# Block products after Strassen's scheme for two of the matrix products of a gated MLP behind windowed attention

## The chip, the core and the metric

The kernel runs on one core of a Trainium2 chip. Its engines are named as in the profile: PE is TensorE, DVE is VectorE, ACT is ScalarE, POOL is GpSimd, and SP is the queue that issues the DMAs. The metric is the device time of one execution in microseconds (us); smaller is better.

## The reference

Windowed causal attention with a linear bias by distance, over 8 batches of 8 heads (576 positions, 64 numbers a head), and behind it, on the 512 numbers a position that the heads give together, a gated MLP with a residual. Cut to what is computed:

```python
scores = scale * q @ k.T                       # 8 batches, 8 heads, 576 x 576
scores = where((rel >= 0) & (rel < 128), scores + bias, -1e9)
x = softmax(scores) @ v                        # per batch: 576 x 512 over all heads
h = gelu(x @ w_in)                             # w_in 512 x 1024
u, v = h[..., :512], h[..., 512:]
v_n = (v - mean) / sqrt(var + 1e-6) * g_ln
v_s = einsum('ts,bsd->btd', w_sg, v_n) + b_sg  # w_sg 576 x 576
return x + (u * v_s) @ w_out                   # w_out 512 x 512
```

## The kernel before

**Number format.** TensorE is fed with rounded fp32 (`fp32r`). To keep more digits, each operand of the MLP is held as a high part and a low part, the low part being what the rounding left over. A product is then three matmuls into the same PSUM tile: high by high, high by low, low by high. The helper `mm3` issues them from three lines, L567, L568 and L569, so these lines appear for every matrix product of the MLP. The split itself is a cast on ACT (high) and a subtraction on POOL or DVE (low).

**Attention.** Two heads make a pair of 128 partitions; there are 32 pairs, four to a batch. A pair `n` is a row of steps with letters: loads `q`, `L` (SP); scores `*` (PE, L248); `A B C G` (DVE: mask, bias, row minimum; L267, L274); `e E f F j` (ACT: exponentials, L283); `R` (DVE: inverse sums); `r s S` (POOL: scaling, L304); transposes `t T` (PE, L314); `X Y` (DVE: copies with a mask, two instructions each, L323); `z P 2 p` (the first 64 positions); `V` (PE: values, L352); `x h k` (ACT: gather, high part, tail of the low part); `l` (POOL: low part, L366).

**MLP of batch b.** The products are kept transposed, features on the partitions. `tt` and `v` give the half that is normalised (moving operand 512 wide), `vg`, `nv..`, `vn` its gelu, mean, variance and split. `u` gives the other half: four blocks of 128 features by two halves of 288 positions, 12 matmuls each, 96 in all; `uc` (ACT, L697) takes a block out of PSUM and `ug` is its gelu. `y` is the product with `w_sg`, and `gm` (DVE, L720) multiplies it out of PSUM with u. `gh` (ACT, L724) and `gl` (POOL, L727) split the gated result. `O` is the product with `w_out`, again 96 matmuls of 288; `oa` (DVE, L750) adds it out of PSUM to the residual, and `D` stores it.

**Order.** One string, `ORDER`, lists all steps of all batches; each engine runs its own steps in that order, and the framework places the semaphores. Attention steps of the next batch stand between the MLP steps of the one before, except in the last batch, where nothing is left to stand between. PSUM has two buffers for each of three uses (`ps_s`, `ps_a` attention, `ps_m` MLP). An MLP tile in `ps_m` is two banks of 288 or 512.

**Buffers.** `vn` (normalised v, high and low) and `g` (gated result, high and low) have places of their own; `u` is a tile of its own; `xs` is x in two parts, four tiles; `xf` is the residual, eight tiles.

Of the kernel before, what the change touches and what calls it, by code (L numbers as in the profile page):

```python
# [21 lines left out]
def attention_gmlp(  # L22
# [402 lines left out]
    xfs, xss = [{} for _ in range(B)], [{} for _ in range(B)]  # L425
# [15 lines left out]
    def add_pair(n):  # L441
# [35 lines left out]
        put("p", "ACT", 0.2, [f"2{n}"], take=[("xf", [f"D{b}{c}"])])  # L477
# [98 lines left out]

    def add_norm(b, key, at, after, rows, done, his, lo):
# [19 lines left out]
        def high():  # L597
            x["hi"] = his()
            for h in x["hi"]:
                nc.scalar.activation(h, x["vg"][0:rows], AF.Copy, scale=x["rs"][0:rows])  # L600

        def low():
            nc.vector.scalar_tensor_tensor(out=lo(), in0=x["vg"][0:rows], scalar=x["rs"][0:rows], in1=x["hi"][0].bitcast(F32), op0=ALU.mult, op1=ALU.subtract)
# [6 lines left out]
        add(k + "h", "ACT", 1.25 if key == "t" else 0.63, at, high, [k + "p", k + "c"] + ([f"y{b - 1}{f}{i}" for f in range(NF) for i in range(2)] if b else [f"-{c}" for c in range(2 * NC)]))  # L610
        add(done, "DVE", 0.68, at, low, [k + "h"], port=True)

    def add_mlp(b):
# [55 lines left out]
        def add_v(t2, at):  # L669
            for i in range(2):  # L670
                t = t2 + i
                take = [("ps_m", [f"vg{b}{t2}", f"vg{b}{t2 + 1}"])]
                if b == 0:
                    for c in range(NC):
                        add(f"w{t}{c}" if c < NC - 1 else f"v{b}{t}", "PE", 0.75, pair_at(c) + OPEN, v_sum(t, [c]), [f"h{c}", f"l{c}", f"-{c}", f"H{c}", f"w{t}{c - 1}" if c else None, f"w{t2}0" if i else None], take=take if c == 0 and i == 0 else [])
                else:
                    add(f"v{b}{t}", "PE", 2.82, at + 2.82 * STRETCH * i, v_sum(t, range(NC)), rows + ([f"v{b}{t2}"] if i else []), take=take if i == 0 else [])
            for i in range(2):
                last = at + 2.82 * STRETCH * i
                add(f"vg{b}{t2 + i}", "ACT", 0.51, last - AHEAD, gelu_v(t2 + i), [f"v{b}{t2 + i}"], table="g", take=[("vg", [f"vn{b}{t2 + i}"])])  # L680
                add_norm(b, f"v{t2 + i}", last, [f"vg{b}{t2 + i}"], P, f"vn{b}{t2 + i}", lambda t=t2 + i: [vn()[:, 0, t, :]], lambda t=t2 + i: vn()[:, 1, t, :])

        def add_u(f, at):
# [10 lines left out]
            def copy():  # L694
                if f == 0:
                    st["u"] = mlp.tile([P, NF, S], F32, name="u")
                nc.scalar.copy(in2(st["u"][:, f, :]), st[f"pu{f}"][:, :, 0:S2])  # L697
# [3 lines left out]
            add(f"uc{b}{f}", "ACT", 0.55, at - AHEAD, copy, [f"u{b}{f}1"] + ([f"uc{b}0"] if f else []), take=[] if f else [("u", [f"gl{b}{k}" for k in range(NF)])])  # L701
            if f == NF - 1:
                add(f"ug{b}", "ACT", 2.05, at, lambda: nc.scalar.activation(st["u"], st["u"], AF.Gelu_apprx_tanh), [f"uc{b}{k}" for k in range(NF)], table="g")

        def add_y(f, at):
            fs = slice(f * P, (f + 1) * P)

            def sums(i):
                def run():
                    if i == 0:  # L710
                        st[f"py{f}"] = ps_m.tile([P, 2, 512], F32, name="ps_m")
                    y, ss, vn, vA = st[f"py{f}"][:, i, 0:S2], halves[i], st["vn"], st["vA"]
                    mm3(y, [((vn[:, 0, t, fs], vn[:, 1, t, fs]), (ws[:, 0, t, ss], ws[:, 1, t, ss])) for t in range(T)], last=False)
                    nc.tensor.matmul(y, vA[:, fs], wsA[:, ss], start=False, stop=False)  # L714
                    nc.tensor.matmul(y, vB[:, fs], wsB[:, ss], start=False, stop=True)  # L715
                return run

            def gate():
                u = st["u"][:, f, :]
                nc.vector.tensor_tensor(in2(u), st[f"py{f}"][:, :, 0:S2], in2(u), ALU.mult)  # L720

            def high():
                st[f"g{f}"] = mlp.tile([P, 2, S], F32R, name="g", bufs=NF)
                nc.scalar.activation(st[f"g{f}"][:, 0, :], st["u"][:, f, :], AF.Copy)  # L724

            def low():
                nc.gpsimd.tensor_tensor(st[f"g{f}"][:, 1, :], st["u"][:, f, :], st[f"g{f}"][:, 0, :].bitcast(F32), ALU.subtract)  # L727

            for i in range(2):
                need = [f"tn{b}", f"nt{b}h"] + [f"vn{b}{t}" for t in range(T)] + (["t-", "b-", "tH"] + [f"w-{c}" for c in range(T)] if b == 0 else [])  # L730
                add(f"y{b}{f}{i}", "PE", 1.87, at + 1.87 * STRETCH * i, sums(i), need + ([f"y{b}{f}0"] if i else []), take=[] if i else [("ps_m", [f"gm{b}{f}"])])
            add(f"gm{b}{f}", "DVE", 0.69, at - AHEAD, gate, [f"y{b}{f}1", f"ug{b}"])
            add(f"gh{b}{f}", "ACT", 0.6, at - AHEAD, high, [f"gm{b}{f}"] + (["bH", "tl"] + [f"i{8 + c}" for c in range(NF)] if b == 0 else []), take=[("g", [f"O{b}{c}" for c in range(NC)])])
            add(f"gl{b}{f}", "POOL", 1.39, at - AHEAD, low, [f"gh{b}{f}"])

        def add_o(c, at):
# [11 lines left out]
            def total():  # L748
                o = x[c]
# [12 lines left out]
            add(f"D{b}{c}", "SP", 0.5, at, lambda: nc.sync.dma_start(out[b, cs, :], x[c]), [f"oa{b}{c}"], lag=2.5)  # L762
# [126 lines left out]
```

## Time and profile before

| what | value |
|---|---|
| median of 3 runs (632.78 to 634.25) | 633.5 us |
| the profiled execution: its own time | 634.58 us |
| its span, first to last instruction | 632.9 us |
| so outside the span | 1.7 us |
| granted TensorE clock, mean | 0.995 |
| instructions | 14839 |
| DMA traffic | 57.24 MB |

A busy share in the profile is the time in which an engine had an instruction running, over the span. For PE the ends of instructions are modelled, since matmuls overlap in its pipeline; the distance from one start to the next is the better measure of what a matmul costs. A row of a group names line, engine and operation, output and input tiles, the shape, the count, then the busy time, the mean of one in ns, and the idle time of the engine ahead of these instructions with what ended it. A row of waits names who waited for whom, the sum in us, how many times, and the longest.

### The profile page before, as it was taken

The page shows a single profiled execution, that of the slowest core. Times are in us where ns is not written, and L with a number is a line of the kernel's source. Part 1 is how long each engine was busy: PE and PEld are TensorE (multiplying, and loading weights), DVE is VectorE, ACT ScalarE, POOL GpSimd, SP SyncE. Part 2 cuts the span into 40 slices and gives each one's busy share as a digit, 9 for nine tenths or more (in the row PEclk, how much of TensorE's full clock was granted, in tenths as well). Part 3 has the DMA queues.
Part 4 walks back from the last instruction along what each step waited for, and adds up shares of the span by engine and source line. Part 5 has one row for each costly group of instructions (what it writes and reads, how often), then busy time and mean ns, then how long its engine had stood idle before and what let it go on. Part 6 is the DMA issues. An engine that isn't in the chain of part 4 may idle for free.

```text
span 632.9 us, 14839 instructions
## 1 busy us (share of the span) xinstructions
PE 602.5 (95%) x5664; PEld 549.7 (87%) x5664; DVE 379.7 (60%) x1297; ACT 369.6 (58%) x1079; POOL 224.6 (35%) x229
## 2 busy tenths in 40 slices
PE   2799899999999999999999999999999999999997
PEld 1577799898999899998999889998899879998896
DVE  4899887465664664548545676546845486633511
ACT  7999687845653467447664586439354465733330
POOL 3666533623073303624053140722325141450220
PEclk9999799999999999999999999999999999999999
DMA  7786321212321520342221422134023512000003
GB/s 249 246 267 217 116 73 46 71 40 79 114 58 42 153 78 2 104 143 99 78 60 40 152 78 78 48 111 150 1 78 103 168 38 80 3 2 20 1 1 132
DMA packets 55931, 57.24 MB, mean 90 GB/s; under 512 B 8498, under 2 KB 45362, under 8 KB 55860
## 3 DMA queue, kind: packets, MB, share of 16 engines
q1 hardware_dynamic: 55860, 56.28, 28.3%
q8 instruction: 45, 0.74, 0.5%
q14 instruction: 26, 0.21, 0.1%
HBM read 46.83 MB, written 9.44 MB: 89 GB/s over the span
## 4 chain that ended last, share of the span: by engine, by line
PE 80%; DVE 8%; ACT 8%; issue 2%; DMA 1%; POOL 1%; POOLq 0%; SPq 0%; ACTq 0%; DVEq 0%
PE ps_m L567 19%; PE ps_m L569 18%; PE ps_m L568 18%; PE ps_s L352 7%; PE ps_a L314 4%; PE ps_s L248 4%; PE ps_a L248 3%; ACT e L283 2%; DVE px L323 2%; PE ps_m L714 1%; PE ps_m L715 1%; ACT e L302 1%; PE ps_m L651 1%; PE ps_m L653 1%; DMA qk<-qkT 1%
## 5 line engine op out<-in xcount | busy, mean ns | idle before, releaser
L283 ACT ACTIVATE e<-e,stats 128x128 f32<-128x128 f32 (+1 forms) x320 | 121.1, 381 | 29.2 <-DVE stats L267 28.8
L304 POOL TENSOR_TENSOR e<-e,rr 128x512 f32<-128x512 f32 (+1 forms) x88 | 73.6, 851 | 129.9 <-DVE rr L296 113.6
L567 PE MATMUL ps_m<-xs,wi 128*128 128x288 f32 x256 | 79.1, 309 | 3.0 <-ACT vg L641 1.8
L567 PE MATMUL ps_m<-ws,vn 128*128 128x288 f32 x256 | 78.2, 306 | 0.0
L567 PE MATMUL ps_m<-g,wo 128*128 128x288 f32 x256 | 78.2, 305 | 0.0
L568 PE MATMUL ps_m<-xs,wi 128*128 128x288 f32 x256 | 76.0, 297 | 0.0
L569 PE MATMUL ps_m<-xs,wi 128*128 128x288 f32 x256 | 76.0, 297 | 0.0
L569 PE MATMUL ps_m<-g,wo 128*128 128x288 f32 x256 | 75.8, 296 | 0.0
L568 PE MATMUL ps_m<-ws,vn 128*128 128x288 f32 x256 | 75.6, 295 | 0.0
L569 PE MATMUL ps_m<-ws,vn 128*128 128x288 f32 x256 | 75.4, 295 | 0.0
L568 PE MATMUL ps_m<-g,wo 128*128 128x288 f32 x256 | 74.9, 293 | 0.5 <-POOL g L727 0.5
L592 POOL TENSOR_TENSOR rs<-rs,mhalf 128x1 f32<-128x1 f32 (+1 forms) x40 | 30.5, 763 | 125.8 <-DVE rs L589 115.1
L366 POOL TENSOR_TENSOR xs<-xf,xs 128x576 fp32r<-128x576 f32 x32 | 45.4, 1427 | 53.3 <-ACT xs L363 51.3
L727 POOL TENSOR_TENSOR g<-u,g 128x576 fp32r<-128x576 f32 x32 | 45.5, 1423 | 50.7 <-ACT g L724 50.6
L323 DVE TENSOR_TENSOR px<-ps_a,m_old 128x512 f32<-128x512 f32 x64 | 43.6, 682 | 31.8 <-PE ps_a L314 21.8
L283 ACT ACTIVATION_READ_ACCUMULATOR e<-e,stats 128x1 f32 (+1 forms) x320 | 60.4, 189 | 0.0
L567 PEld LDWEIGHTS ps_m<-xs,wi 128*128 128x128 f32 x256 | 48.8, 191 | 8.8 <-ACT vg L641 2.5
L750 DVE TENSOR_TENSOR xf<-ps_m,xf 128x576 f32<-128x576 f32 x32 | 23.7, 749 | 52.4 <-PE ps_m L569 52.3
L567 PE MATMUL ps_m<-wi,xs 128*128 128x512 f32 x128 | 52.4, 409 | 1.4 <-ACT vg L641 1.4
L248 PE MATMUL ps_s<-qk 64*64 64x192 f32 (+2 forms) x632 | 40.3, 344 | 14.2 <-DMA qk<-qkT 10.3
L352 PE MATMUL ps_s<-px,vt 128*64 128x128 f32 (+1 forms) x972 | 51.2, 259 | 0.3 <-DVE px L323 0.2
L352 PEld LDWEIGHTS ps_s<-px,vt 128*64 128x64 f32 x972 | 47.2, 137 | 3.9 <-issue 2.1
(120 smaller groups left out, 1522.0 us busy)
## 6 DMA issues: line engine op xcount, KB each, us to landing
qk<-qkT SPq DMA_DIRECT2D x32, 576.0 KB, 4.1
vt<-v_in SPq DMA_DIRECT2D x64, 256.0 KB, 3.4
outT<-xf SPq DMA_DIRECT2D x32, 288.0 KB, 2.8
wst<-w_in SPq DMA_DIRECT2D x8, 512.0 KB, 5.0
vt<-v_in SPq DMA_DIRECT2D x64, 32.0 KB, 2.9
wst<-w_out SPq DMA_DIRECT2D x4, 512.0 KB, 4.5
wst<-w_sgT SPq DMA_DIRECT2D x4, 288.0 KB, 6.0
vd<-v_in SPq DMA_DIRECT2D x64, 16.0 KB, 2.9
```

The source lines that it names most:

```text
L248: return lambda: nc.tensor.matmul(dst, qk[js, 0, q0:q0 + R], qk[js, 1, k0:k1], start=True, stop=True)
L283: nc.scalar.activation(x, x, AF.Exp, bias=self.nm[0:n, i:i + 1], scale=-1.0, accum_out=self.sm[0:n, i:i + 1])
L304: nc.gpsimd.tensor_tensor(x, x, self.rr[0:n, i:i + m].rearrange("p (m o) -> p m o", o=1).broadcast_to([n, m, c]), ALU.mult)
L314: burst([lambda t=t: nc.tensor.transpose(ct[:, t * P:(t + 1) * P], self.pr[j][:, t, :], ident) for t in range(T)])
L323: nc.vector.tensor_tensor(xv[:, :, :, i, :], cv, m.rearrange("p (t h c) -> p t h c", t=1, h=1).broadcast_to([P, T, 2, R]), ALU.mult)
L352: return lambda: nc.tensor.matmul(x1[heads[j], q0 + lo // 2 * R if t < 0 else q0 + t * R:q0 + (hi + 1) // 2 * R], block, px[j][:, (half * ...
L366: nc.gpsimd.tensor_tensor(lo_of(self.xs), self.xf, hi_of(self.xs).bitcast(F32), ALU.subtract)
L567: nc.tensor.matmul(dst, ah, bh, start=(first and i == 0), stop=False)
L568: nc.tensor.matmul(dst, ah, bl, start=False, stop=False)
L569: nc.tensor.matmul(dst, al, bh, start=False, stop=(last and i == n - 1))
L592: nc.gpsimd.tensor_tensor(x["rs"][0:rows], x["rs"][0:rows], mhalf[0:rows], ALU.pow)
L727: nc.gpsimd.tensor_tensor(st[f"g{f}"][:, 1, :], st["u"][:, f, :], st[f"g{f}"][:, 0, :].bitcast(F32), ALU.subtract)
```

## The change

The products `O` of batches 1 to 7 and `u` of batches 2 to 7 are cut into 2 by 2 blocks (weights 256 by 256, moving side 256 by 288) and formed from seven block products in place of eight. A block product is 12 matmuls of 288 columns (two row blocks, two inner blocks, three for the parts). The constant `FAST = 2` says from which batch `u` is done this way. Batch 0 keeps both old forms, batch 1 keeps the old `u`.

What that takes, by step names (`b` is the batch, `n` the number of the block product, 1 to 7):

- `U{b}{n}` and `O{b}{n}` (PE): the block products. They share two PSUM tiles. Products 1, 6, 7, 4 go through the one and 5, 3, 2 through the other; 6, 7, 4 and 3 are added to what is in the tile, and each product is taken out before the next goes into the same tile.
- `ue` (four on ACT, three on DVE) and `oa` (seven on DVE, in place of four) take them out. Their row length is again 576.
- `ut` (4 a batch) and `gt` (4 a batch): differences of blocks of x and of the gated result, on DVE from SBUF to SBUF. `uh`, `ul` and `gh`, `gl` split them; that is 4 splits a batch that were not there for `u`, and 7 in place of 4 for `O`. `gl6` is on DVE, the others on POOL; two of them a batch (`gl1`, `gl2`) and `ul6` are cut in two instructions.
- Sums of weights, once: `Us0`..`Us9` on POOL and `ks0`..`ks9` on DVE (128x512 each), `Uh`, `kh` (8 on ACT) and `Ul`, `kl` (8 on DVE) for the split. Three of the four sums of a matrix stay in three tiles `sum`; the fourth replaces a block of the weights. Both matrices use the same three tiles, so the sums are stored in DRAM (`Ud`, `kd`: 6 stores of 512 KB) and loaded back when the other matrix is at work (`lu`, `lo`: 18 loads of 512 KB each). The loads stand in SP's queue with those of q, k, v and the stores of the output.
- Buffers: `vn` and the split blocks share one tile `region` of four slots, with a fifth slot in `g` and `spare`. So a block of the gated result may only be written when `y` has read the part of `vn` in that slot, and `vn` of the next batch only when the block product that reads the slot is done. `u` and the residual (two sets for even and odd batches) are fixed tiles.
- The first two `y` of a batch are cut in two (`ya` over the first half of the positions, then `y`), `v` of batches 2 to 7 is cut around the `U`, and `D` stores a block of 256 by 288, four a batch as before.
- `ORDER` is written anew.

Counted in the two programs, PE has 4418 instructions before and 4262 after, DVE 1299 and 1415, ACT 761 and 814, POOL 234 and 302, SP 279 and 321. (The weight loads of PE are not in these counts, and the profile counts some small matmuls of the attention twice; those of 288 columns are the same in both.)

The diff, cut to its core:

```diff
+    store = [dram.tile([P, 3, 2, 2, 2 * P], F32, name=f"store{i}") for i in range(2)]
+    def load_sums(i, number):
+        return lambda: nc.sync.dma_start(sums[i].bitcast(F32), store[number][:, i])
...
+    SLOT_USE = {0: 5, 1: 6, 2: 4, 3: 7}
...
+        def add_fast_u(at):
+            def less(n, a, c):
+                return lambda: nc.vector.tensor_tensor(u(*place[n]), a, c, ALU.subtract)
+            def put(n):
+                add(f"uh{b}{n}", "ACT", 0.69, at, high(n), [f"ut{b}{n}"] + freed[n])
+                add(f"ul{b}{n}", "POOL", 1.42, at, low(n), [f"uh{b}{n}"])
...
+            def product(n, key, first):
+                def run():
+                    if key not in st:
+                        st[key] = ps_m.tile([P, 2, 512], F32, name="ps_m")
+                    for m in range(2):
+                        ms = slice(m * P, (m + 1) * P)
+                        dst = st[key][:, m, 0:S2]
+                        for c in range(2):
+                            for k, (g, h) in enumerate(((0, 0), (0, 1), (1, 0))):
+                                nc.tensor.matmul(dst, left(n, g, c)[:, ms], right(n, h, c), start=first and c == 0 and k == 0, stop=c == 1 and k == 2, skip_group_check=True)
+                return run
+            def take_out(key, i, j, engine):
+                def run():
+                    p = st[key][:, :, 0:S2]
+                    if engine == "ACT":
+                        nc.scalar.copy(u(i, j), p)
+                    else:
+                        nc.vector.tensor_tensor(u(i, j), p, u(i, j), ALU.add)
+                return run
+            for n, i in BY.items():
+                add(f"lu{b}{i}", "SP", 0.5, at - AHEAD, load_sums(i, 0), [f"O{b - 1}{n}", "Ud0", "Ud1", "Ud2", f"kd{i}"], lag=3.5)
...
+        def add_fast(at):
+            put(1, gm[0:2])
+            add(f"gt{b}1", "DVE", 0.75, at, less(5, "12", 1), [f"gl{b}1"] + gm[0:2], port=True)
+            put(5, [f"gt{b}1"])
+            add(f"gt{b}2", "DVE", 0.75, at, less(6, 3, 5), [f"gl{b}5"] + gm[2:4], port=True)
+            put(6, [f"gt{b}2"])
...
+            for n, key, first, i, j in ((1, "pa", True, 0, 0), (5, "pb", True, 1, 1), (6, "pa", False, 0, 1), (3, "pb", False, 0, 1), (7, "pa", False, 1, 1), (2, "pb", True, 0, 0), (4, "pa", False, 1, 0)):
+                add(f"O{b}{n}", "PE", 1.6, at, product(n, key, first), [f"gl{b}{n}", before.get(key), before.get("pe")] + (["kl2", "kl0", "kl1", "kl3"] if b == 1 else [f"lo{b}{BY[n]}"] if n in BY else []), take=[] if key in before else [("ps_m", [users[key]])])
+                add(f"oa{b}{n}", "DVE", 0.76, at, total(n, key, i, j), [f"O{b}{n}"])
...
     ORDER = """
...
-        E19 R19 Y18 s19 S19 z18 O30 P18 r19 t19 oa30 218 V18 p18 k16 T19 X19 x18 O32 h18 Y19 l18 oa33 z19 V19 oa32 P19
...
+        gh35 gl35 gm32 V18 gm33 r19 gt32 gt33 t19 O31 X19 gh37 gh33 gl37 T19 z19 O35 Y19 P19 gh36 gl33 gh32 k17 z18
```

What the new list does shows best on the engines themselves. First PE in the `u` of batch 4. Before, a half of a block of 128 features is twelve rows that take the four tiles of x in turn (`xs`), all into one tile of PSUM, and eight such halves make `u`:

```order
L567 MATMUL ps_m_4457<-xs_4086,wi_141 128x288
L568 MATMUL ps_m_4457<-xs_4086,wi_141 128x288
L569 MATMUL ps_m_4457<-xs_4086,wi_141 128x288
L567 MATMUL ps_m_4457<-xs_4387,wi_141 128x288
L568 MATMUL ps_m_4457<-xs_4387,wi_141 128x288
L569 MATMUL ps_m_4457<-xs_4387,wi_141 128x288
```

After, on PE at the same place, products 5, 6 and the first half of 3 stand behind each other (product 1 went into tile 4651 some steps earlier, with a `V` of attention behind it; `sum` are the tiles that the loads fill, `fifth` and `spare` the fifth slot):

```order
L867 MATMUL ps_m_4698<-region_1025,sum_1478 128x288 x12
L867 MATMUL ps_m_4651<-fifth_2168,sum_1479 128x288 x4
L867 MATMUL ps_m_4651<-spare_143,sum_1479 128x288
L867 MATMUL ps_m_4651<-fifth_2168,sum_1479 128x288 x5
L867 MATMUL ps_m_4651<-spare_143,sum_1479 128x288
L867 MATMUL ps_m_4651<-fifth_2168,sum_1479 128x288
L867 MATMUL ps_m_4698<-xs_4403,sum_1480 128x288 x3
L867 MATMUL ps_m_4698<-xs_4417,sum_1480 128x288 x3
```

So product 6 goes into tile 4651 again, one product of 12 matmuls after `U41` and `V20`, and product 3 into tile 4698 one product after the 5: the taking-out of a product has the length of one other product.

Second, DVE at the end of batch 4, from the second mask step of attention pair 22 (`Y22`) to the last of the four additions to the residual. Before:

```order
L323 TENSOR_TENSOR px_5159<-ps_a_5119,m_old_85 128x4x2x64
L323 TENSOR_TENSOR px_5159<-ps_a_5119,m_own_84 128x4x2x64
L295 TENSOR_SCALAR rr_5193<-stats2_139 128x10
L296 RECIPROCAL rr_5193<-rr_5193 128x10
L750 TENSOR_TENSOR xf_3820<-ps_m_5137,xf_3820 128x576
L750 TENSOR_TENSOR xf_4416<-ps_m_5166,xf_4416 128x576
L323 TENSOR_TENSOR px_5236<-ps_a_5198,m_old_85 128x4x2x64
L323 TENSOR_TENSOR px_5236<-ps_a_5198,m_own_84 128x4x2x64
L323 TENSOR_TENSOR px_5264<-ps_a_5231,m_old_85 128x4x2x64
L323 TENSOR_TENSOR px_5264<-ps_a_5231,m_own_84 128x4x2x64
L750 TENSOR_TENSOR xf_4319<-ps_m_5239,xf_4319 128x576
L750 TENSOR_TENSOR xf_4114<-ps_m_5301,xf_4114 128x576
```

After, from the last gate product of the batch (`gm43`) on: `oa41`, `gt42`, the two mask pairs of pair 23, `oa45`, `gl46`, `gt43` and `gt44`, `oa46`, and the first difference of batch 5 (`ut55`):

```order
L908 TENSOR_TENSOR u_144<-ps_m_5142,u_144 128x576
L1018 TENSOR_TENSOR xf00_145<-ps_m_5165,xf00_145 128x2x288
L977 TENSOR_TENSOR u_144<-u_144 128x2x288
L334 TENSOR_TENSOR px_5239<-ps_a_5202,m_old_87 128x4x2x64
L334 TENSOR_TENSOR px_5239<-ps_a_5202,m_own_86 128x4x2x64
L334 TENSOR_TENSOR px_5256<-ps_a_5234,m_old_87 128x4x2x64
L334 TENSOR_TENSOR px_5256<-ps_a_5234,m_own_86 128x4x2x64
L1018 TENSOR_TENSOR xf01_146<-ps_m_5242,xf01_146 128x2x288
L973 TENSOR_TENSOR region_1025<-u_144,region_1025 128x576
L977 TENSOR_TENSOR u_144<-u_144 128x2x288 x2
L1018 TENSOR_TENSOR xf00_145<-ps_m_5165,xf00_145 128x2x288
L833 TENSOR_TENSOR u_144<-xf10_147 128x2x288
```

Between the additions there now stand the differences and the one split on DVE, all reading SBUF twice.

Third, SP where batch 2 goes over into batch 3. Before, the queue held loads of q, k, v and stores only. After, the loads of the sums stand in it, ahead of the loads of v for pair 16 (`vt`) and of a load of q and k:

```order
L657 DMA sum_1479<-store1_158 128x1024
L657 DMA sum_1480<-store0_157 128x1024
L657 DMA sum_1478<-store0_157 128x1024
L241 DMA vt_3530<-v_in 128x4x128
L242 DMA vt_3530<-v_in 64x128
L241 DMA vt_3530<-v_in 128x4x128
L242 DMA vt_3530<-v_in 64x128
L244 DMA vd1_127<-v_in 64x64 x2
L233 DMA qk_3584<-qkT 128x1152
L1031 DMA outT<-xf00_145 128x2x288
L657 DMA sum_1479<-store0_157 128x1024
```

Each of the loads waits there for the product that last read the old content of its tile.

More of the change, by code (lines that the diff above doesn't have):

```diff
@@ L476, in add_pair @@
         put("2", "PE", 0.12, [f"P{n}", f"L{n}"])
[L477 removed]
+        put("p", "ACT", 0.2, [f"2{n}"] + ([] if b < 2 else [f"D{b - 2}{c}"] if b == 2 else [f"D{b - 2}{c // 2 * 2 + j}" for j in range(2)]))
         put("t", "PE", 0.45, [f"s{n}"], take=[("ps_a", [f"X{n}"])])
@@ L705, in add_y, with sums @@
         def add_y(f, at):
             fs = slice(f * P, (f + 1) * P)
-            def sums(i):
+            def sums(i, ts, tail, first, last):
                 def run():
-                    if i == 0:
+                    if first and i == 0:
                         st[f"py{f}"] = ps_m.tile([P, 2, 512], F32, name="ps_m")
[L712 to L715, printed above, removed]
+                    y, ss, vA = st[f"py{f}"][:, i, 0:S2], halves[i], st["vA"]
+                    mm3(y, [((vn(0, t, f), vn(1, t, f)), (ws[:, 0, t, ss], ws[:, 1, t, ss])) for t in ts], first=first, last=last and not tail)
+                    if tail:
+                        nc.tensor.matmul(y, vA[:, fs], wsA[:, ss], start=False, stop=False)
+                        nc.tensor.matmul(y, vB[:, fs], wsB[:, ss], start=False, stop=last)
@@ new lines, in attention_gmlp @@
+        F22 y410 E22 y400 h21 y401 f22 y411 j22 *23 R22 gm41 s22 gm40 y420 q25 l21 A23 e23 B23 r22 h20 S22 y421 E23
+        C23 G23 l20 j23 gh41 t22 gm42 T22 F23 gl41 y430 f23 R23 X22 O41 r23 s23 gt41 y431 Y22 S23 gh45 k21 gl45 t23
+        gm43 V22 oa41 gh43 gt42 gh42 gh46 gl42 T23 X23 O45 k20 Y23 gl43 z23 V23 oa45 gl46 gt43 z22 O46 gt44 gh47 P22
+        P23 gl47 223 222 oa46 lu51 O43 p23 x23 p22 ut55 x22 h23 ut57 *24 h22 oa43 gh44 l22 A24 D41 L24 O47 e24 B24
+        gl44 j24 C24 E24 O42 oa47 l23 uh55 G24 O44 F24 lu52 oa42 k23 f24 q26 D40 *25 k22 uh57 oa44 R24 A25 r24 tt5 s24
@@ L855, in attention_gmlp @@
+        ue75 lo70 nv17p nv07c U73 ue76 lo71 nv07p D63 uh74 nv17h ul74 U77 ue73 lo72 nv07h U72 ue77 vn71 vn70 U74 ue72
+        ue74 ug7 v72 vg72 nv27b v73 nv27c nv27p ya700 vg73 nv27h nv37b ya701 nv37c ya710 nv37p ya711 vn72 nv37h vn73
+        y700 y701 y710 gm70 y711 y720 gm71 gh71 gl71 y721 gt71 y730 gm72 y731 gh75 gl75 O71 gm73 gt72 O75 gt73 gh76
+        gh73 gl76 gh77 oa71 gl73 gh72 oa75 O76 gl77 O73 oa76 gl72 O77 gt74 oa73 gh74 D71 O72 oa77 gl74 D73 O74 oa72
+        D70 oa74 D72
     """
```

382 lines of the change are left out of this document (286 added, 96 removed).

## The prediction

> **What bounds the kernel now.** I read the page's busy shares first, then the stages as a table, then PE's own rows in time, then who made PE wait. The page's first part:
>
> ```profile
> PE 602.5 (95%) x5664; PEld 549.7 (87%) x5664; DVE 379.7 (60%) x1297; ACT 369.6 (58%) x1079; POOL 224.6 (35%) x229
> PEclk9999799999999999999999999999999999999999
> HBM read 46.83 MB, written 9.44 MB: 89 GB/s over the span
> ```
>
> PE is near full, the others are not, and its granted clock dips in one of 40 slices only. A mean can hide stages, so here are four stretches cut near the starts of `tt1`, `tt2`, `tt4`, `tt5` and `tt7` (us; busy time and count for each engine, granted clock, DMA):
>
> ```profile
> 137.40:222.90 85.50, 84.64 (x770) 77.57 (x770) 50.78 (x148) 41.32 (x114) 27.07 (x28) 1.00 0.30 90
> 353.40:426.60 73.20, 73.20 (x711) 67.66 (x710) 45.31 (x156) 43.34 (x129) 24.26 (x25) 1.00 0.30 92
> 426.60:524.00 97.40, 94.93 (x884) 85.52 (x883) 60.47 (x214) 56.35 (x173) 32.59 (x35) 1.00 0.29 90
> 572.60:632.90 60.30, 54.42 (x363) 50.78 (x361) 20.10 (x36) 14.25 (x20) 9.89 (x9) 1.00 0.10 40
> ```
>
> Batch 3 (second row) has PE busy in all of its 73.2 us; DVE has 45.3 of them, ACT 43.3, POOL 24.3. The last row is the last batch's MLP, alone, with PE free for 5.9 us. Busy is not full speed, so I look at the starts. In a `u` block, the first and the last of 59 rows:
>
> ```profile
> 302.16 0.29 PE L568 MATMUL ps_m<-xs,wi 128*128 128x288 f32 x1
> ...
> 309.85 0.29 PE L569 MATMUL ps_m<-xs,wi 128*128 128x288 f32 x1
> ```
>
> These are 58 steps in 7.69 us, 0.1326 us from start to start, without a hole. What PE waits for:
>
> ```profile
> PE ps_s L248 <- DMA qk<-qkT: 10.3, 1, 10.3
> PE ps_m L567 <- ACT vg L641: 3.2, 3, 1.4
> PE ps_s L248 <- DVE stats L267: 2.7, 3, 1.1
> PE ps_m L567 <- ACT u L697: 1.2, 1, 1.2
> ```
>
> The long one is the very first load. Behind it a few waits of one or two us each are all there is. So after the start the kernel is PE's stream of matmuls, and taking matmuls out shortens it by 0.1326 us apiece, as long as nothing else takes PE's place.
>
> **What the change removes.** `O` of seven batches and `u` of six lose 12 of 96 matmuls each: 13 x 12 = 156, and that is also the difference of the instruction counts of the two programs on PE. 156 x 0.1326 = 20.7 us. The Trainium skill, "TensorE: Matmul & The Clock Gate", section "Back-to-back issue gap", gives columns over 2.4 GHz plus 2.5 ns for a warm matmul, by estimate 0.1225 us here and 19.1 us in all, which would make the sum 620.6 in place of 619.0; the trace is 8% above it, and I go by the trace.
>
> **What it adds, off PE.** The prices, from groups and from the chain of work:
>
> ```profile
> L595 DVE SCALAR_TENSOR_TENSOR vg<-vg,mv,gb 128x512 f32<-128x512 f32 x32 | 26.9, 850 | 0.0
> L720 DVE TENSOR_TENSOR u<-ps_m,u 128x576 f32<-128x576 f32 x32 | 23.9, 752 | 40.1 <-PE ps_m L715 35.3 <-ACT u L703 4.7
> L697 ACT COPY u<-ps_m 128x576 f32<-128x576 f32 x32 | 20.2, 635 | 24.0 <-PE ps_m L569 24.0
> L724 ACT ACTIVATE g<-u 128x576 fp32r<-128x576 f32 x32 | 21.5, 680 | 34.5 <-DVE u L720 34.5
> L727 POOL TENSOR_TENSOR g<-u,g 128x576 fp32r<-128x576 f32 x32 | 45.5, 1423 | 50.7 <-ACT g L724 50.6
> ```
>
> A batch of 2 to 7 gets on DVE 4 `ut`, 4 `gt`, 3 `ue`, 3 more `oa` and `gl6`: 15 x 0.75 = 11.3 us. ACT gets 4 `uh` and 3 more `gh`: 7 x 0.68 = 4.8. POOL gets 4 `ul` and 2 more `gl`: 6 x 1.42 = 8.5. Against batch 3's row, PE falls to 73.2 - 24 x 0.1326 = 70.0, DVE rises to 56.6 (81%), ACT to 48.1, POOL to 32.8. None reaches PE, so the work itself is covered by matmuls; the cover is 13 us of DVE a batch, not more. Batch 1 is the fullest: 8 `gt`, `oa`, `gl6`, and of the weights' sums 10 `ks` and 8 splits, 26 x 0.75 = 19.5 us on the 50.8 of the first row, 70 of 84. Within it the steps between `ya110` and `U21` lie closest. What DVE spends over the whole span on the scores' minima (L267, then L274: 32 pairs) and on the mask steps (L323: 64):
>
> ```profile
> 0.00:632.90 632.90, 74.13 (x640) 0.99 0.29 90
> 0.00:632.90 632.90, 36.66 (x128) 0.99 0.29 90
> 0.00:632.90 632.90, 80.85 (x128) 0.99 0.29 90
> ```
>
> That is 3.46 us a pair and 1.26 a mask step. Between the two places the new list has five pairs' scores (17.3), nine mask steps (11.4), 24 instructions of 0.75 (`gm`, `oa`, `gt`, `gl6`, `ut`, `ks`, `kl`: 18.0), and some 8 us of norms and inverses: 55 us. PE has there seven products, ten `y` steps and `ya`, four `V` and sets of scores, two `v`, `tt2` and ten transposes: 54 us by its steps of 1.6, 0.133 a matmul and the like, an estimate as the 55 is. DVE has no slack there, and I expect PE to wait: from nothing (DVE works ahead of the section) to 5 us (seven products, each behind one 0.75 instruction). I take the middle, 2.5, because the two sums are equal. POOL's `Us` (10 instructions of 512 columns, under 1.42 each, so under 14 us) lie beside `O0` and `u1`, 25.6 us of PE.
>
> **The DMAs.** 6 stores and 36 loads of 512 KB, 22 MB on 57. What such a size takes to land, beside the loads that stand in the same queue, and how long SP's queue is held today:
>
> ```profile
> wst<-w_in SPq DMA_DIRECT2D x8, 512.0 KB, 5.0
> qk<-qkT SPq DMA_DIRECT2D x32, 576.0 KB, 4.1
> SPq L762 <- DVE xf L750: 185.2, 14, 46.1
> ```
>
> The queue stands behind an output add for up to 46 us now and PE never waits for a load after the first. The new loads wait for a product that has read the tile, and the loads of q, k, v queue behind them. `lu41` for instance is free to go after `O46`, and `U46` comes after `tt4` (1.9), two `v` (5.6), `U41`, `V20`, `U45` (5.0) and attention steps, over 12 us later against 5.0 of landing; `lo` has the whole of `y` (15 us). In the last batch `lu71` stands behind `D62`, which waits for `oa64`; then come `tt7`, two `v`, two products: 10.7 us. Cost between zero and 2 us for each of six batches, if half of the loads slipped by 4; I take zero, since the spacing is twice the landing.
>
> **The new waits.** A PSUM tile used to be taken out while a block of 24 matmuls (3.2 us) or 28 ran in the other; now while 12 run, 1.59 us. Taking out is 0.64 on ACT or 0.75 on DVE. So 0.8 us of room is left for what stands ahead of it in that engine's queue, and who waits for it is PE itself, with all its attention work behind. Today the 120 tiles of `ps_m` (15 a batch: 4 `u`, 2 `v`, 1 `t`, 4 `y`, 4 `o`) cost PE 3.2 + 1.2 = 4.4 us in waits, 0.037 each. There are 91 products now. Lower end: nothing more, 0. Upper end: one mask step ahead of each, which by
>
> ```profile
> 151.66 1.21 DVE px L323 x2
> ```
>
> is 1.21, 0.4 us over the room, 36 us in all. I take today's 0.037 x 91 = 3.4, since in most places of the new list a piece of attention (`V`, scores, transposes) stands between a product and the next one in its tile. In the fence of DVE's list after `gm43`, `oa45` and `gl46` stand behind two mask steps: from the end of `y431`, 0.75 x 3 for `gm`, `oa`, `gt`, two mask steps 2.4, `oa45` 0.75 and `gl46` 0.75 give 6.2 us, and PE has there a transpose, `V22`, a transpose, `O45`, `V23`, about 6.6. It just fits.
>
> Also late next: `region`. The splits of the gated result may start only when `y` has read the slot; `O` of product 1 goes into the fifth slot for that reason and is done by then.
>
> **The tail,** where nothing stands between. The chain of work in the last us of today:
>
> ```profile
> 611.78 0.77 DVE u L720
> 612.58 0.69 ACT g L724
> 613.34 1.43 POOL g L727
> ...
> 629.01 0.76 DVE xf L750
> ```
>
> From the last add's start to the end are 3.9 us, so of the 5.9 without PE 2.0 are waits. In the new list, after the last `y`: `gm73`, `gt72`, `gt73`, `gl76`, `oa71` on DVE, 5 x 0.76 and the drain of some 0.2 make 4.0, and `O76` waits for `oa71`; `O71` and `O75` fill 3.2 of it. PE waits 0.8 there. `gt74` and `oa73` ahead of `O72` cost 0.4 in the same way; `gl74` just makes it. 1.2 us in place of 2.0: -0.8.
>
> **Sum.** 634.6 (this execution's own time; its span is 632.9) - 20.7 + 2.5 + 3.4 - 0.8 = 619.0. The median of the runs is 1.1 below this execution, so **618 us**.
>
> **Rivals.**
>
> *DVE and POOL block each other.* Most of what is added reads SBUF twice on DVE (77 instructions) or on POOL (68). The trace has rows on that, in time, one engine below the other:
>
> ```profile
> 364.02 2.39 POOL L304 TENSOR_TENSOR e<-e,rr 64x128 f32<-64x128 f32 x3 [2.33 <-DVE rr L296]
> ...
> 364.81 2.14 DVE L603 SCALAR_TENSOR_TENSOR vA<-vg,rs,vA 64x512 fp32r<-64x512 f32 x1 [0.23 <-ACT vA L600]
> ...
> 589.65 0.76 DVE vn L603
> ```
>
> The same operation takes 0.76 with POOL idle and 2.14 while POOL runs. L595's mean of 0.85 against 0.75 says 0.1 us an instruction on average. The new ones pay 77 x 0.1, and with POOL at 225 + 68 (6 x 8.5, 2.8 in batch 1, 14 for the sums) of 613 us in place of 225 of 633, a third denser, 77 x 0.13 = 10 us; they stand in chains that PE waits for (`gt`, `gl6`), so up to all of it reaches PE: 618 + 9 = 627. This is also a rule of the Trainium skill, "SBUF — State Buffer", section "SBUF: two separate sides": a DVE instruction with two SBUF inputs and a GpSimd instruction that reads SBUF hold a port pair exclusively, and the second blocks until the first is done. The row of 2.14 agrees with it. By that rule in full the time is 627; 618 has only what the means of 0.75 hold.
>
> *The taking-out becomes the bound, and the kernel gets slower.* The place is PE's wait on `ue` and `oa`. The gain is gone when each of 91 products waits 20.7 / 91 = 0.23 us more. If half have a mask step and one 0.75 ahead, they are late by 1.21 + 0.75 - 0.8 = 1.16: 46 x 1.16 = 53, and 618 - 3.4 + 53 = 668; a quarter gives 641. Against it: four of the seven `ue` are on ACT at 69% load, and the list seldom has two such in a row.
>
> *Loads late.* If the `lu` of six batches come 2 us late, +12: 630.
>
> *It doesn't do what it says.* The count on PE excludes that.
>
> **Chances.** Likeliest, 611 to 622: 0.62. Port or a full DVE, 622 to 628: 0.17. Loads or several together, 628 to 632: 0.07, and 0.02 of no change. Slower by the taking-out: 0.06. Under 611, if the new list also mends waits of the start (the page's first slices have PE at 2 and 7 tenths): 0.06. The range 611 to 628 leaves out two in ten. A change of 0.2%, 1.3 us, is about what can be told from none here: faster 0.92, same 0.02, slower 0.06.
>
> **What will show it.** Rows of L867 and L1012 with 0.133 us from start to start and 156 fewer of 288 columns; batch stretches of 70 us with PE busy in all; DVE near 80%. Waits of PE on `ps_m` for L874, L876, L1018 would be the taking-out; DVE instructions of L977 and L833 over 0.8 in the mean the blocking; PE waiting on `sum` for DMA the loads. I am wrong if these waits sum to over 10 us.

## The result and the profile after

The changed kernel takes 616.8 us (median of four runs, 616.28 to 618.58) against 633.6: a ratio of 0.9741, 95% interval 0.9718 to 0.9763. The forecast was 618, 611 to 628. The profiled execution took 618.58 with a span of 616.9, where the prediction's sum against the profiled execution before came to 619.0. So the total is right to 0.4 us; the terms behind it are not all right, and one of them is right in size for a wrong reason.

The page of the changed kernel, its busy shares, the granted clock and the DMA total:

```profile
PE 585.2 (95%) x5508; PEld 529.5 (86%) x5508; DVE 457.0 (74%) x1413; ACT 399.0 (65%) x1132; POOL 298.2 (48%) x297
PEclk9999999999999999999999999999999999999999
HBM read 65.70 MB, written 12.58 MB: 127 GB/s over the span
```

156 instructions fewer on PE, which is still 95% busy; DVE has 77 us more, POOL 74. By stages: `tt1` to `tt2`, `tt2` to `tt3`, `tt4` to `tt5`, and `tt7` to the end, each cut at the first matmul (columns as before: us, then busy time and count of PE, weight loads, DVE, ACT, POOL, then clock, DMA share, GB/s):

```profile
128.80:209.20 80.40, 78.48 (x751) 71.15 (x749) 63.21 (x193) 48.88 (x145) 33.76 (x33) 0.98 0.36 121
209.20:280.20 71.00, 68.09 (x675) 62.21 (x673) 57.55 (x168) 49.89 (x136) 33.05 (x33) 1.00 0.42 126
350.40:421.10 70.70, 70.63 (x687) 64.64 (x685) 54.88 (x173) 44.14 (x131) 32.98 (x34) 1.00 0.40 126
559.70:616.90 57.20, 51.40 (x336) 47.44 (x336) 29.65 (x50) 19.08 (x27) 17.96 (x17) 0.99 0.23 74
```

A middle batch (third row) takes 70.7 where 70.0 was worked out and 73.2 stood before; PE is busy in all of it, DVE in 78% (81% forecast). (The row that the prediction calls batch 3 also runs from `tt4` to `tt5`, so it is batch 4; batch 3 took 73.3 and the sums hold for both.) The second row is the odd one: PE is idle for 2.9 us. The waits of PE between 100 us and the start of `tt3`, before and after (us in all, times, longest):

```profile
PE ps_m L567 <- ACT vg L641: 0.7, 1, 0.7
PE ps_s L352 <- DVE px L323: 0.2, 1, 0.2
```

```profile
PE ps_m L1012 <- DVE xf L1018: 1.9, 1, 1.9
PE ps_a L338 <- DVE px L334: 0.9, 1, 0.9
PE ps_m L867 <- ACT vg L748: 0.6, 1, 0.6
PE ps_a L325 <- DVE stats L278: 0.5, 1, 0.5
PE ps_m L867 <- DVE vg L765: 0.4, 1, 0.4
PE ps_a L345 <- ACT p L341: 0.3, 1, 0.3
PE ps_s L363 <- PE ps_a L338: 0.2, 1, 0.2
```

0.9 us became 4.8. From there to 559 us, where each batch has products in `u` and in `O`, the same view of the changed kernel lists no wait of PE at all (before, to 572 us: 2.4). So the new waits stand in batches 1 and 2, and not where the products are dense.

The largest wait, 1.9, has a chain that the timeline shows (start, us, engine, line; the rows of PE between are left out):

```profile
262.67 0.39 POOL L315 TENSOR_TENSOR e<-e,rr 64x128 f32<-64x128 f32 x1
262.92 5.02 DVE L973 TENSOR_TENSOR region<-u,region 128x576 fp32r<-128x576 f32 x1
263.02 1.42 POOL L377 TENSOR_TENSOR xs<-xf,xs 128x576 fp32r<-128x576 f32 x1
...
264.41 1.41 POOL L973 TENSOR_TENSOR region<-u,region 128x576 fp32r<-128x576 f32 x1
...
265.78 0.79 POOL L973 TENSOR_TENSOR fifth<-u,fifth 128x288 fp32r<-128x288 f32 x1
...
266.53 0.79 POOL L973 TENSOR_TENSOR spare<-u,fifth 128x288 fp32r<-128x288 f32 x1
...
267.86 1.41 DVE L1018 TENSOR_TENSOR xf<-ps_m,xf 128x576 f32<-128x576 f32 x2
...
268.66 3.46 PE L1012 MATMUL ps_m<-region,sum 128*128 128x288 f32 x24 [1.94 <-DVE xf L1018]
```

The row of 5.02 is `gl26`, an instruction of 0.75. POOL works through five instructions without a gap, and DVE's ends 0.6 us after the last of them. Behind it in DVE's queue stand `oa21` and `oa25` (L1018), and PE waits for the first of these.

### The profile page after: what moved, and what is told of

Same layout as the page of the kernel before. It is cut to its first block, busy times and chain, and to the rows that moved or that the text cites. A ratio compares the mean times of both kernels' runs of the same rounds, so it can differ in the third digit from the quotient of the medians.

```text
span 616.9 us, 14945 instructions
## 1 busy us (share of the span) xinstructions
PE 585.2 (95%) x5508; PEld 529.5 (86%) x5508; DVE 457.0 (74%) x1413; ACT 399.0 (65%) x1132; POOL 298.2 (48%) x297
## 4 chain that ended last, share of the span: by engine, by line
PE 72%; DVE 13%; ACT 11%; issue 2%; DMA 1%; POOL 1%; ACTq 0%; SPq 0%; DVEq 0%; POOLq 0%
PE ps_m L1012 11%; PE ps_m L867 11%; PE ps_m L578 10%; PE ps_m L579 9%; PE ps_m L580 9%; PE ps_s L363 7%; ACT e L294 4%; DVE px L334 3%; PE ps_a L325 3%; PE ps_s L259 3%; PE ps_a L259 3%; DVE e L278 2%; PE ps_m L902 1%; PE ps_m L903 1%; PE ps_m L758 1%
## 5 line engine op out<-in xcount | busy, mean ns | idle before, releaser
L294 ACT ACTIVATE e<-e,stats 128x128 f32<-128x128 f32 (+1 forms) x320 | 121.4, 381 | 27.5 <-DVE stats L278 27.0
L315 POOL TENSOR_TENSOR e<-e,rr 128x512 f32<-128x512 f32 (+1 forms) x88 | 73.8, 856 | 69.5 <-DVE rr L307 55.1
L578 PE MATMUL ps_m<-ws,region 128*128 128x288 f32 x256 | 78.0, 305 | 0.4 <-ACT u L802 0.3
L579 PE MATMUL ps_m<-ws,region 128*128 128x288 f32 x256 | 75.6, 295 | 0.0
L580 PE MATMUL ps_m<-ws,region 128*128 128x288 f32 x256 | 75.6, 295 | 0.0
L294 ACT ACTIVATION_READ_ACCUMULATOR e<-e,stats 128x1 f32 (+1 forms) x320 | 60.2, 188 | 0.0
L377 POOL TENSOR_TENSOR xs<-xf,xs 128x576 fp32r<-128x576 f32 x32 | 47.4, 1484 | 14.4 <-ACT xs L374 14.4
L363 PE MATMUL ps_s<-px,vt 128*64 128x128 f32 (+1 forms) x972 | 53.5, 263 | 0.7 <-DVE px L334 0.3
L363 PEld LDWEIGHTS ps_s<-px,vt 128*64 128x64 f32 x972 | 49.0, 140 | 5.7 <-DVE px L334 2.4
L967 ACT ACTIVATE region<-u 128x576 fp32r<-128x576 f32 x35 | 23.3, 683 | 47.0 <-DVE u L977 20.7
L578 PE MATMUL ps_m<-wi,xs 128*128 128x512 f32 x128 | 52.9, 413 | 0.7 <-ACT vg L748 0.7
L973 POOL TENSOR_TENSOR region<-u,region 128x576 fp32r<-128x576 f32 x28 | 39.9, 1432 | 26.5 <-ACT region L967 21.6
L580 PE MATMUL ps_m<-wi,xs 128*128 128x512 f32 x128 | 50.6, 395 | 0.6 <-POOL xs L377 0.6
L578 PEld LDWEIGHTS ps_m<-ws,region 128*128 128x128 f32 x256 | 48.3, 189 | 2.7 <-issue 1.1
L579 PE MATMUL ps_m<-wi,xs 128*128 128x512 f32 x128 | 50.5, 395 | 0.0
L579 PEld LDWEIGHTS ps_m<-ws,region 128*128 128x128 f32 x256 | 48.2, 188 | 0.1
L580 PEld LDWEIGHTS ps_m<-ws,region 128*128 128x128 f32 x256 | 48.1, 188 | 0.0
L1018 DVE TENSOR_TENSOR xf<-ps_m,xf 128x576 f32<-128x576 f32 x49 | 36.5, 750 | 12.8 <-PE ps_m L1012 12.6
L334 DVE TENSOR_TENSOR px<-ps_a,m_own 128x512 f32<-128x512 f32 x64 | 43.5, 680 | 0.0
```

The lines of the kernel that those rows point to most:

```text
L294: nc.scalar.activation(x, x, AF.Exp, bias=self.nm[0:n, i:i + 1], scale=-1.0, accum_out=self.sm[0:n, i:i + 1])
L315: nc.gpsimd.tensor_tensor(x, x, self.rr[0:n, i:i + m].rearrange("p (m o) -> p m o", o=1).broadcast_to([n, m, c]), ALU.mult)
L334: nc.vector.tensor_tensor(xv[:, :, :, i, :], cv, m.rearrange("p (t h c) -> p t h c", t=1, h=1).broadcast_to([P, T, 2, R]), ALU.mult)
L363: return lambda: nc.tensor.matmul(x1[heads[j], q0 + lo // 2 * R if t < 0 else q0 + t * R:q0 + (hi + 1) // 2 * R], block, px[j][:, (half * ...
L377: nc.gpsimd.tensor_tensor(lo_of(self.xs), self.xf, hi_of(self.xs).bitcast(F32), ALU.subtract)
L578: nc.tensor.matmul(dst, ah, bh, start=(first and i == 0), stop=False)
```

## The experiments

Eleven kernels, each an edit of the changed one. Theory A in the expectations is that PE's stream of matmuls sets the time and the added side work is covered. Against it stand the blocking of DVE and POOL, the taking-out of products from PSUM (`ue`, `oa`), and the loads.

**Twelve matmuls back.**

```diff
-                        for c in range(2):
+                        for c in (0, 1, 0, 1) if n == 1 else (0, 1):
...
-                        for f in range(2):
+                        for f in (0, 1, 0, 1) if n == 1 else (0, 1):
```

> Product 1 of each set is computed twice over (the second time from zero), so that the 156 matmuls come back and everything else of the change stays. Theory A (PE's stream of matmuls sets the time, the added side work is covered): 156 x 0.1326 = 20.7 on 616.8, that is 637.5 (636 to 639), slower than the kernel before by what the added side work and the new list cost, about 4. Rival B (PE waits for the side work, DVE above all): the second pass falls into those waits, 626 to 633. In the rows, A wants the same few waits of PE as in the changed kernel and DVE's busy time unchanged.

Measured: 633.2 us (632.6 to 634.0), a ratio of 0.9994 (0.9984 to 1.0003) to the kernel before. That is between the two expectations: the 156 matmuls cost 16.4. The stretches from `tt3` to `tt4` and from `tt4` to `tt5` say how:

```profile
280.80:354.20 73.40, 73.40 (x713) 67.79 (x709) 53.99 (x174) 45.52 (x133) 34.38 (x34) 1.00 0.42 131
354.20:427.80 73.60, 73.59 (x710) 67.72 (x708) 55.12 (x173) 44.16 (x131) 32.96 (x34) 1.00 0.38 120
```

Against 70.2 and 70.7: 3.2 and 2.9 for 24 matmuls, where 24 x 0.1326 is 3.2. In middle batches a matmul costs its full price. In batch 2 24 of them cost 0.9, because the 1.9 wait is gone here, and in the last batch (to its last matmul) 1.9 in place of 3.2, because a wait of 0.8 for L967 is gone there. So with all matmuls back the added side work and the new list cost nothing that shows in the medians, and the change gives 16.8 of 20.7. Nothing in sum is not nothing in each part. The granted clocks of the runs (means 0.9972 here, 0.9954 before) hide some 1.1 us, an estimate. In the traces the waits behind matmuls of the MLP are 1.9 shorter than before, and attention's steps take 3.5 us longer (added up as in the section on the prediction).

**One and four matmuls fewer in each product.** The matmuls with the low part of the weights, in one quarter of each product and in all of it:

```diff
+                            terms = ((0, 0), (0, 1), (1, 0))[:2 if m and c else 3]
-                            for k, (g, h) in enumerate(((0, 0), (0, 1), (1, 0))):
+                            for k, (g, h) in enumerate(terms):
```

> Each of the 91 products leaves out one matmul (a low part of the weights for a quarter of it): 91 fewer, by full price 12.1. If the changed kernel still has room, 604.7 to 607; if it already stands at the bend that the kernel with 8 of 12 showed (14.1 for 364, 0.039 each), 613.3. I expect 606 to 610: the waits set in bit by bit.

> Each of the 91 products leaves out the matmuls with the low part of the weights (8 matmuls in place of 12): 364 fewer, and 1.06 us in place of 1.59 to take a product out in. Theory A: PE is still the bound, 364 x 0.1326 = 48.3, so 568.5; with DVE then at 54 of 63 us a batch I allow 3 to 15 us of new waits: 572 to 584. Rival (the taking-out, or DVE as a whole, is already near its limit): more than half of the 48 is eaten by waits of PE on ps_m for L876 and L1018 and on region for L973, 593 or more.

Measured: 609.5 (609.24 to 610.61) and 602.7 (602.35 to 603.58). A matmul is worth 0.105 us on the way up, 0.080 for the first 91 on the way down, 0.039 over the first 364, of a price of 0.133. The changed kernel stands where the line bends: some more can be taken off, and soon PE waits. In the kernel with 8 of 12 PE waits in many small pieces, for nearly every other engine:

```profile
PE ps_m L1012 <- DVE xf L1018: 4.4, 4, 2.8
PE ps_m L867 <- ACT u L874: 4.1, 7, 0.9
PE ps_m L1012 <- ACT region L967: 3.3, 2, 1.8
...
PE ps_a L338 <- DVE px L334: 3.0, 5, 0.9
PE ps_s L363 <- DVE px L334: 2.2, 9, 0.3
PE ps_m L867 <- DVE u L876: 1.7, 3, 0.9
```

34.2 us of the 48.3 are missing there. Two more kernels ask whose they are. The first only takes a quarter of the columns out:

```diff
-                    p = st[key][:, :, 0:S2]
+                    p, w = st[key][:, :, 0:S2 // 4], u(i, j)[:, :, 0:S2 // 4]
...
-                    o = x[i][:, :, halves[j]]
+                    o = x[i][:, :, halves[j]][:, :, 0:S2 // 4]
```

> As the kernel with 8 matmuls of 12, and each taking-out of a product (L874, L876, L1018) only does a quarter of its columns (the rest of u and of the output stays without that product), about 0.2 in place of 0.75 us. If the taking-out is what ate the 34 us that were missing there (602.7 in place of 568.5), most of it comes back: 575 to 592. Rival (the attention's chain over DVE and ACT and the splits eat it): 595 or more.

Measured: 590.7 (588.69 to 591.57): 12.0 back. The second has POOL's low parts as writes of zero too (the edit stands below):

> As the kernel with 8 matmuls of 12 and a quarter of the taking-out (590.7), and POOL's low parts for the products are writes of zero as well. 22 us of the 48.3 are still missing there. If POOL's splits (their length and their blocking of DVE) hold them: 575 to 585. Rival (the attention's chain of scores, minima, exp, masks holds them): 587 to 591.

Measured: 579.9 (579.58 to 580.11): another 10.8. So of the missing 34.2, taken away in this order, the taking-out holds 12.0, POOL's low parts with their blocking 10.8, and 11.4 are left for the attention's chain and all else. The rival that the taking-out becomes the bound explains a third of it, and only below the time that the change reaches.

**The loads.** `load_sums` issues nothing:

```diff
-        return lambda: nc.sync.dma_start(sums[i].bitcast(F32), store[number][:, i])
+        return lambda: None
```

> The 36 loads of the sums of weights are left out (the products take what lies in the three tiles). Theory A: the loads are hidden, 616.8 within 1 us either way. Rival (the loads, or q, k and v behind them in SP's queue, come late): 605 to 612, by 2 us for each of six batches.

Measured: 618.0 (615.76 to 618.35), a ratio of 0.9739 (0.9719 to 0.9759) against the changed kernel's 0.9741. 18.9 MB of loads cost nothing.

**POOL's low parts without reading.**

```diff
-                        nc.gpsimd.tensor_tensor(lo, u(*place[n])[:, fs], hi[:, fs].bitcast(F32), ALU.subtract)
+                        nc.gpsimd.memset(lo.bitcast(F32), 0.0)
...
-                        engine.tensor_tensor(lo, u(n)[:, fs], hi[:, fs].bitcast(F32), ALU.subtract)
+                        if engine is nc.gpsimd:
+                            engine.memset(lo.bitcast(F32), 0.0)
+                        else:
+                            engine.tensor_tensor(lo, u(n)[:, fs], hi[:, fs].bitcast(F32), ALU.subtract)
```

> POOL's low parts for the products (L829, L973 on POOL) become writes of zero, which read no SBUF and wait for no high part; the low part on DVE (gl6) and all else stay. Theory A: blocking by POOL costs PE only the one wait of about 2 us near 266 us, and little more: 613 to 616.5; the means of L977 and L833 on DVE fall from 0.83 towards 0.76, and DVE's busy time by some 8 us without the time following. Rival (blocking in full): the 9.7 us by which DVE's rows stand over their medians come off the time, 607 or less.

Measured: 615.5 (613.72 to 616.24), 1.3 below the changed kernel. DVE's busy time falls by 7.9 us, to 449.1. `gl26` now:

```profile
263.35 0.74 DVE L976 TENSOR_TENSOR region<-u,region 128x576 fp32r<-128x576 f32 x1
```

and batch 2 takes 68.5 in place of 71.0. The mean of twelve of the `ut` (L833) falls from 0.811 to 0.761. But `gt` (L977 in the changed kernel, L980 here) stays where it was, at 0.833 before:

```profile
L980 DVE TENSOR_TENSOR u<-u 128x576 f32<-128x576 f32 x28 | 23.1, 838 | 1.3 <-ACT fifth L967 0.8
```

In the trace its two longest, 1.8 and 2.1 us, overlap POOL's other instructions (L377 and L315), which still read. The edit also frees POOL from the high part that it waited for. So it bounds from above what the blocking by the new low parts costs: 1.3 us, and not 9. What the blocking by L315 and L377 costs stays in the time.

**`gl6` on POOL, and `gl26` alone earlier in the list.** Two ways to be rid of the one long row.

```diff
-                if n == 6:
+                if n == 0:
```

> The low part of product 6, the one that is on DVE, goes to POOL like the others. Theory (the 5.02 us row is DVE shut out while POOL works through its queue, and it is what cost PE 1.9 near 266 us): that wait goes, L1018 no longer makes PE wait there; against it the low part takes 1.42 in place of 0.75 and stands in POOL's queue, which the tail of the last batch pays with about 1. So 615 to 617, within 0.3% of the changed kernel. Rival (the row was only a late input): the wait stays and POOL's longer chain makes it 618 to 622.

Measured: 618.4 (617.97 to 620.12), ratio 0.9766 (0.9748 to 0.9783): no gain. Batch 2 falls by some 0.4 to 70.6: of the wait of 1.9 for L1018 0.6 is left, and a wait of 0.7 for ACT (L294) is new behind it. The last batch but one grows by 1.1, with a wait of 0.8 for L1018 that is new, and the last one, to its last matmul, by 0.9, with a new wait of 0.5 for POOL's low part and one of 1.0 for L967 where 0.8 stood: the low part is late by POOL's queue. The other way moves one step:

```diff
-        gm22 R15 s15 T14 y231 Y14 S15 gh25 gl25 V14 gm23 gt22 gt23 t15 T15 gh26 gh27 X15 O21 gl27 gh23 Y15 O25 r15 l12
-        z14 z15 P14 V15 gl26 P15 gh22 oa21 gl23 oa25 215 214 gl22 O26 p15 p14 x14 x15 h15 gt24 O23 h14 ut35 k13 oa26
+        gm22 R15 s15 T14 y231 Y14 S15 gh25 gl25 V14 gm23 gt22 gt23 t15 T15 gh26 gh27 gl26 X15 O21 gl27 gh23 Y15 O25 r15 l12
+        z14 z15 P14 V15 P15 gh22 oa21 gl23 oa25 215 214 gl22 O26 p15 p14 x14 x15 h15 gt24 O23 h14 ut35 k13 oa26
```

> Only the list: the low part of product 6 of batch 2 on DVE stands ahead of the mask step X15 in place of behind V15, so that it asks for SBUF before POOL's row of five starts. Theory: it takes 0.75 in place of 5.02, PE's wait of 1.9 near 266 goes, and the mask step is late by about half a us: 614.5 to 616.5. Rival (what is late only moves on, as in the run with that part on POOL): 616.8 to 618.5.

Measured: 614.0 (613.25 to 615.81), a ratio of 0.9681 (0.9662 to 0.9700): faster than the changed kernel's 0.9741 (0.9718 to 0.9763) with intervals apart. In its timeline and its stretches:

```profile
257.45 0.76 DVE L973 TENSOR_TENSOR region<-u,region 128x576 fp32r<-128x576 f32 x1
...
258.17 1.43 POOL L973 TENSOR_TENSOR region<-u,region 128x576 fp32r<-128x576 f32 x1 [2.32 <-ACT region L967]
```

```profile
206.00:274.90 68.90, 67.86 (x674) 62.13 (x672) 52.25 (x168) 50.20 (x137) 32.12 (x33) 1.00 0.46 138
```

DVE asks 0.7 us before POOL does and is through in 0.76; batch 2 is 2.1 shorter. By the medians the version gains 2.8 on the changed kernel; the granted clocks of the runs (means 0.9975 and 0.9965) make some 0.6 of it, an estimate. Among the versions that leave nothing of the computation out this is the fastest.

**The sums of w_out on POOL.** `("k", wo, nc.vector, "DVE"` becomes `("k", wo, nc.gpsimd, "POOL"`.

> The ten sums of w_out (L620) go from DVE to POOL: 7 us less DVE in batch 1, 13 us more POOL. Theory (batch 1 after ya110 is short of DVE, which is what the 3 us of PE's waits between 183 and 222 us are): those waits fall by 1 to 2, 614.5 to 616.5. Rival (those waits are latencies of the chain through DVE and not its load): 616.8, or later if the sums come late on POOL.

Measured: 619.7 (619.49 to 621.42), slower. The waits of batch 1 are all there still:

```profile
PE ps_m L1012 <- DVE xf L1018: 2.3, 1, 2.3
PE ps_a L338 <- DVE px L334: 0.9, 1, 0.9
PE ps_a L325 <- DVE stats L278: 0.7, 2, 0.5
PE ps_m L867 <- ACT vg L748: 0.7, 1, 0.7
```

So the waits of batch 1 don't follow DVE's load, as far as these 7 us show; which latencies of the chain hold them was not taken apart.

**`O` alone by seven products.** `FAST = 8`, no sums of wi, no stores and loads, and in the list the half blocks of `u` in the places of its products.

> Only the output sums by seven products; u of batches 2 to 7 by eight as before (72 matmuls back), without its subtractions, splits, sums of wi, stores and loads. Theory: 72 x 0.1326 = 9.5 on 616.8 makes 626.3, less what the side work for u costs PE now, which I put at 0 to 3: 623 to 626.5. Rival (the side work for u eats its gain): 617 to 621.

Measured: 627.3 (626.53 to 628.55). `u` brings 10.5 of the medians' difference, for 72 matmuls worth 9.5: in full. `O` brings 6.3, for 84 worth 11.1. What is missing belongs to the half with `O`: to its side work in batches 1 and 2, where this kernel shows the wait of 1.9 on the taking-out as well, or to the new list, which it shares. Which of the two was not separated.

## Why the prediction was right

**Matmuls, -20.7: right.** The price holds in the rows after. A product each of `O` and of `u`, merged by the timeline:

```profile
262.34 1.76 PE L1012 MATMUL ps_m<-region,sum 128*128 128x288 f32 x12
...
292.37 1.86 PE L867 MATMUL ps_m<-region,sum 128*128 128x288 f32 x12
```

The first: less the 0.29 of the last matmul, 11 steps in 1.47, 0.134 each. The second ends in a distance that is not a matmul's. The matmuls put back cost 3.2 a middle batch, as worked out.

**The dense section of batch 1, +2.5: right in size, wrong in reason.** Of the six small rows above five lie there, 2.5 us (the 0.4 stands behind `U21`). The prediction's ground was that DVE has 55 us of work there and PE 54. Taking 7 us off DVE in batch 1, 2 of them in the section itself, changed none of the rows by more than 0.2, and the kernel with twelve matmuls back has all of them as large.

**The hand-back of PSUM, +3.4: the wrong term.** The 0.037 of each product was a mean of waits that had other causes (most of it `vg`), and it was multiplied by 91. From `tt3` to `tt7` the products cost PE no wait that the view lists. Two waits on L1018 did appear, 1.9 and 0.9: the one behind `gl26`, and `tt7` behind `O64`, where no attention is left to stand between. The room of 0.8 us was worked out rightly; the list keeps it.

**What the sum did not have: attention's steps on PE.** From `tt0` on, the time from each matmul of attention (scores, transposes, values, copies) to the start of the next matmul came to 118.5 us before and 126.5 after, added up from the trace. The matmuls of the MLP, 144 fewer in that part, fell from 424.5 to 403.9 us: 19.1 is the price of the 144, and 1.2 are waits that are gone.

Of attention's 8.0 us 3.0 are waits (5.0 behind its matmuls, 2.0 before). Some 1.6 are the stretch at half the clock (below): from `tt1` to `tt2` attention takes 24.4 here and 22.8 in the kernel without loads, which has no such stretch. The remaining 3.4 are distances too short for a wait row. The kernel with twelve matmuls back has 2.6 of these, so most of them come with the new list and the side work, and not with the missing matmuls; which steps hold them stays open.

The balance of the two profiled executions is then: 20.7 for the matmuls, 1.5 more on the MLP, 2.2 on the start up to `tt0` (where the stretch at half the clock is gone), less 8.0 on attention and 0.4 behind the start of the last matmul, which makes 16.0. The prediction had 20.7, less 5.9 in waits, and 0.8 on the tail: 15.6. That the two agree to 0.4 is luck.

**The tail, -0.8: wrong, 0.** The wait that the prediction names is there, behind `gh76` on ACT and not behind `oa71`:

```profile
604.17 3.43 PE L1012 MATMUL ps_m<-region,sum 128*128 128x288 f32 x24 [0.81 <-ACT region L967]
...
612.64 0.76 DVE xf L1018
```

0.8 of the 1.2 came, though by another engine. The term left out two other waits, 0.9 for L1018 ahead of `tt7` and 0.7 for `vg`: the waits of PE in the last batch sum to 2.4, and to 2.0 before. From the start of the last addition to the end it is now 4.3 us, 3.9 before. The two stretches have the same 5.8 and 5.9 us without PE.

**Loads, 0: right,** by the kernel without them.

**The blocking.** The signs that the prediction named as its proof are all there:

```profile
L977 DVE TENSOR_TENSOR u<-u 128x576 f32<-128x576 f32 x28 | 22.9, 833 | 7.3 <-POOL spare L973 6.7
L973 DVE TENSOR_TENSOR region<-u,region 128x576 fp32r<-128x576 f32 x7 | 10.3, 1477 | 0.1
L833 DVE TENSOR_TENSOR u<-xf,u 128x576 f32<-128x576 f32 x12 | 9.7, 811 | 0.1
```

Over their medians of 0.75 the new instructions of L977, L973 and L833 took 9.7 us too long, and 10 had been worked out. The rival's price was right and its reach wrong: it put up to all of that on PE, and the one wait of PE that the timeline ties to it is the 1.9. That DVE's queue had slack elsewhere fits this and was not shown by itself. The rule cited from the Trainium skill, "SBUF — State Buffer", section "SBUF: two separate sides", is borne out by the row of 5.02 and the 0.76 of the same step asked for earlier.

**The clock** gave 1.7 us that no term had. It is the difference of the half-clock stretches of the two profiled executions. Before and after:

```profile
70.40:77.20 6.80, 6.05 (x46) 5.75 (x47) 4.99 (x11) 3.17 (x8) 2.24 (x2) 0.50 0.50 158
```

```profile
199.80:203.20 3.40, 3.40 (x43) 3.28 (x44) 0.56 (x1) 0.28 (x2) 1.70 (x2) 0.50 0.69 229
```

6.8 us at half speed lose 3.4, 3.4 lose 1.7.

## What to carry to other kernels

When the engine that bounds a kernel got less to do here, its price per instruction held until the cover of the side work was used up; a run with the work put back and one with more taken off show where on that bend a version stands, and here it stands at the beginning of it. A mean over waits is no price: ask of each wait what caused it before multiplying. And a blocked instruction is worth a look in the timeline even where the groups' means look harmless: one step moved in the list brought 2.8 us.

## What the runs showed of the hardware

DVE's instruction with two SBUF inputs did not get its turn between two instructions of POOL: it waited out all five, 4.4 us from its start to the end of the last, and then ran.

The half-clock stretches between the start and the last microseconds are 3.4 us long or twice that, and each of them stands at a pause of PE. In the changed kernel PE had idled 1.2 us in the 3.4 us ahead (waits of 0.9 and 0.3); in the kernel with the sums of w_out on POOL a wait of 2.3 us for L1018 was followed by

```profile
270.60:274.00 3.40, 3.40 (x17) 3.40 (x16) 3.40 (x3) 0.00 (x0) 2.68 (x2) 0.51 0.00 0
```

and in the kernel with 8 of 12 matmuls a stretch of 6.8 us begins within a pause of 2.8 us. Of seven kernels with that wait near 265 us (1.9 to 2.8 us), three (the third is the one with 11 of 12) show such a stretch at it and four do not; the five kernels where it is gone or under 1 us show none there. The two waits near 198 us, of 0.8 to 0.9 and 0.3 us, stand in all twelve kernels with the change, and only the changed one and the one with POOL's writes of zero show a stretch behind them. So a wait of PE can cost 1.7 or 3.4 us more, and its length alone doesn't decide it; what does stays open. The Trainium skill, "TensorE: Matmul & The Clock Gate", section "What's actually happening", has a window of 3.4 us that runs freely and lowers the clock after an idle window; the lengths agree, and in two kernels here the clock fell behind 1.2 us of idling in 3.4 us, about a third of such a window.
